# A causal convolution and a two-layer GELU block: both matmuls as pairs of 64-row tiles, the convolution moved to VectorE

## The chip, the cores and the metric

The kernel runs on one core of one Trainium2 chip. A core has a matrix engine (TensorE, "PE" in the profile, with its weight loads listed apart as "PEld"), a vector engine (VectorE, "DVE"), a scalar engine with function tables (ScalarE, "ACT"), a general engine (GpSimd, "POOL") and a queue engine that issues transfers (SyncE, "SP"). Each runs its own list of instructions in order; they meet only through semaphores. The metric is the device time of one execution in microseconds, as the median of several runs.

## The reference

Inputs, all float32: `x` of 8 x 4096 x 192, `weight` of 8 x 7, `moe_w_in` of 192 x 2048, `moe_w_out` of 2048 x 192.

```python
w = softmax(weight, axis=-1)                    # 8 heads x 7 taps
x_pad = concatenate([zeros((B, 6, D)), x], 1)   # causal: six rows of zeros in front
# channel d belongs to head d // 24
conv[b, s, d] = sum over k of w[d // 24, k] * x_pad[b, s + k, d]
h = conv.reshape(32768, 192) @ moe_w_in
g = 0.5 * h * (1 + erf(h / sqrt(2)))            # exact GELU
out = (g @ moe_w_out).astype(float32)           # 32768 x 192
```

So every token (a row of 192 channels) is mixed with the six before it in its sequence, head by head, and then goes through 192 -> 2048 -> GELU -> 192. The two matmuls hold nearly all the arithmetic.

## The kernel before, in words

The 32768 tokens go through in 64 blocks of 512 (`TB`), and a block in four tiles of 128 tokens. The order of all work is written out by hand: each engine has one list, and the blocks are software-pipelined within it.

*Load.* SP loads a block of x (384 KB) into one of three buffers `x_tok`, 128 tokens on the partitions (line 435), and stores finished output blocks (line 441). POOL casts each tile to bf16 (`x_tokb`, line 163).

*Convolution.* It is done by TensorE. At the start, VectorE builds for each of the 8 heads a banded matrix `S_ext` of 128 x 256 that holds the seven taps along its diagonals (lines 231 and 233), out of a shifted identity `bigI2` and the softmax weights. For a tile of 128 tokens `conv_st` runs, for each head, one matmul with the tile (line 363) and one with the tile before it, for the six tokens that reach back (line 373). The 24 channels of a head are the columns of the weight load, and four heads go to four column tiles of 32 (`tile_position=(0, 32 * jj)`). The result has channels on the partitions: 24 of each 32, four heads in each of two halves. ScalarE copies it as bf16 to `x2T` (line 299).

*Matmul 1.* For each 128 of the 2048 hidden units (`i` = 0..15) two matmuls add into one accumulator `hp` of 128 x 512: `winTA` with the first four heads and `winTB` with the other four (lines 395 and 402). Both use all 128 rows of the array, of which 4 x 24 = 96 hold data and the others zeros, as in `x2T`.

*GELU.* ScalarE takes a sigmoid of 1.5957... times `hp` into `tT` (line 313), and VectorE multiplies `tT` with `hp` into `gT`, bf16 (line 245): the sigmoid form that stands in for the exact GELU. There are four `hp` accumulators.

*Matmul 2.* For each tile of 128 tokens, 16 matmuls of 192 columns (line 341) add up over the 2048 hidden units; `gT` is the weight side, `woutT` streams. VectorE copies the 128 x 192 sums out (lines 258 and 272).

*Order on TensorE.* In block `bb`, behind each matmul-1 step `i` from 2 on stand four matmuls of matmul 2 of the block before; two tiles of the next block's convolution stand behind step 3, and two behind step 11. Matmul 1 waits for the multiply four steps back (`S_MULT`), the convolution for POOL's cast (`S_XCAST`) and ScalarE's copy (`S_EVAC`), matmul 2 for VectorE's copy out (`S_OCPY`).

*Start.* POOL clears six buffers, then issues the load of the tap weights (line 132) and of both weight matrices. VectorE and ScalarE compute the softmax on one partition (lines 182 to 209), TensorE spreads it over the partitions (line 326), VectorE copies that (line 219) and builds `S_ext`, and only then the first convolution and the first matmul 1 start.

Of the kernel before, what the change touches and what calls it, by code (L numbers as in the profile page):

```python
# [9 lines left out]

SIG_ALPHA = 1.5957691216057308


def bass_lightweight_conv__then__act_gelu_exact_kernel(
# [12 lines left out]
    GRP = D // H  # L27
    assert H == 8 and GRP == 24 and KS == 7
    NTOK = B * SEQ
    TB = 512  # L30
    assert NTOK % TB == 0 and SEQ % TB == 0
    NB = NTOK // TB
    NST = NTOK // 128
    STB = SEQ // 128
    NF = F // 128
    assert NF % 2 == 0
    NCH = NF
    NWDMA = 9

    NX = 3  # L40
    R = 8
    RT = 4
    HZ = 4
# [17 lines left out]

    with es:
        S_ext = sbt("S_ext", [128, H * 256], BF16)
        winTA = sbt("winTA", [128, F], BF16)
        winTB = sbt("winTB", [128, F], BF16)
        woutT = sbt("woutT", [128, NF * C], BF16)
        bigI2 = sbt("bigI2", [128, 448], BF16)
        wsb = sbt("wsb", [1, 64], F32)
        wmax = sbt("wmax", [1, 8], F32)
        wsh = sbt("wsh", [1, 64], F32)  # L70
        wex = sbt("wex", [1, 64], F32)
        wsum = sbt("wsum", [1, 8], F32)
        winv = sbt("winv", [1, 8], F32)
        wrow = sbt("wrow", [1, 64], F32)
        ones1 = sbt("ones1", [1, 128], F32)
        wbc = sbt("wbc", [128, 64], F32)
        x_tok = [sbt("x_tok%d" % i, [128, 4 * D], F32) for i in range(NX)]
        x_tokb = [sbt("x_tokb%d" % i, [128, D], BF16) for i in range(R)]
        x2T = [sbt("x2T%d" % i, [128, 2 * TB], BF16) for i in range(2)]
        tT = [sbt("tT%d" % i, [128, TB], BF16) for i in range(RT)]  # L80
        gT = [sbt("gT%d" % i, [128, NF * TB], BF16) for i in range(2)]
        o_sb = [sbt("o_sb%d" % i, [128, 4 * C], F32) for i in range(2)]
        pc = [pst("pc%d" % i, [128, 256]) for i in range(2)]
        hp = [pst("hp%d" % i, [128, TB]) for i in range(HZ)]
        obk = [pst("obk%d" % i, [128, 192]) for i in range(2)]
        S_WDMA = sem("S_WDMA")
        S_WSB = sem("S_WSB")
        S_POOLP = sem("S_POOLP")
        S_DVEP = sem("S_DVEP")
        S_ACTP = sem("S_ACTP")  # L90
        S_PEP = sem("S_PEP")
        S_XDMA = [sem("S_XDMA%d" % i) for i in range(NX)]
        S_ODMA = [sem("S_ODMA%d" % i) for i in range(2)]
        S_XCAST = sem("S_XCAST")
        S_CONV = sem("S_CONV")
        S_EVAC = sem("S_EVAC")
        S_MM1P = sem("S_MM1P")
        S_SIG = sem("S_SIG")
        S_MULT = sem("S_MULT")
        S_MM2S = sem("S_MM2S")  # L100
        S_OCPY = sem("S_OCPY")
# [3 lines left out]
        def ap(t, off, pat):  # L105
            return bass.AP(t, off, pat)

        def x_dram_ap(bb):
            return ap(xt, bb * TB * D, [[D, 128], [128 * D, 4], [1, D]])

        def out_dram_ap(bb):
            return ap(outt, bb * TB * C, [[C, 128], [128 * C, 4], [1, C]])

        def xtok_ap(slot):
            return ap(x_tok[slot], 0, [[4 * D, 128], [D, 4], [1, D]])

        def osb_ap(slot):
            return ap(o_sb[slot], 0, [[4 * C, 128], [C, 4], [1, C]])

        POOLP_MEMSETS = 6  # L120
        POOLP_TOTAL = POOLP_MEMSETS + 1

        @block.gpsimd
        def _(g):
            g.memset(winTA[:, :], 0.0).then_inc(S_POOLP)  # L125
            g.memset(winTB[:, :], 0.0).then_inc(S_POOLP)  # L126
            g.memset(bigI2[:, :], 0.0).then_inc(S_POOLP)
            g.memset(ones1[:, :], 1.0).then_inc(S_POOLP)
            g.memset(x2T[0][:, :], 0.0).then_inc(S_POOLP)
            g.memset(x2T[1][:, :], 0.0).then_inc(S_POOLP)  # L130
            g.wait_ge(S_POOLP, POOLP_MEMSETS)
            g.dma_start(
                wsb[0:1, 0 : H * KS], ap(wt, 0, [[H * KS, 1], [1, H * KS]])
            ).then_inc(S_WSB, 16)
            g.affine_select(
                out=bigI2[:, 6:134],
                in_=bigI2[:, 6:134],
                compare_op=ALU.not_equal,
                fill=1.0,
                base=0,  # L140
                pattern=[[-1, 128]],
                channel_multiplier=1,
            ).then_inc(S_POOLP)
            for j in range(4):
                g.dma_start(  # L145
                    winTA[32 * j : 32 * j + GRP, :],
                    ap(wint, GRP * j * F, [[F, GRP], [1, F]]),
                ).then_inc(S_WDMA, 16)
            for j in range(4):
                g.dma_start(  # L150
                    winTB[32 * j : 32 * j + GRP, :],
                    ap(wint, (4 * GRP + GRP * j) * F, [[F, GRP], [1, F]]),
                ).then_inc(S_WDMA, 16)
            g.dma_start(
                ap(woutT, 0, [[NF * C, 128], [C, NF], [1, C]]),
                ap(woutt, 0, [[C, 128], [128 * C, NF], [1, C]]),
            ).then_inc(S_WDMA, 16)
            for s in range(NST):
                bb, j = divmod(s, 4)
                g.wait_ge(S_XDMA[bb % NX], 16 * (bb // NX + 1))  # L160
                if s >= R:
                    g.wait_ge(S_CONV, s - R + 2)
                g.tensor_copy(  # L163
                    x_tokb[s % R][:, :], x_tok[bb % NX][:, j * D : (j + 1) * D]
                ).then_inc(S_XCAST)

        dvep = [0]

        def dve_inc(ins):
            ins.then_inc(S_DVEP)  # L170
            dvep[0] += 1
            return dvep[0]

        dve_final = []

        @block.vector
        def _(v):
            dve_inc(v.memset(pc[0][:, :], 0.0))
            dve_inc(v.memset(pc[1][:, :], 0.0))
            v.wait_ge(S_WSB, 16)  # L180
            cnt = dve_inc(
                v.tensor_reduce(  # L182
                    wmax[0:1, 0:H],
                    ap(wsb, 0, [[64, 1], [KS, H], [1, KS]]),
                    mybir.AxisListType.X,
                    ALU.max,
                )
            )
            v.wait_ge(S_DVEP, cnt)
            for h in range(H):  # L190
                cnt = dve_inc(
                    v.tensor_scalar(  # L192
                        wsh[0:1, KS * h : KS * h + KS],
                        wsb[0:1, KS * h : KS * h + KS],
                        wmax[0:1, h : h + 1],
                        None,
                        ALU.subtract,
                    )
                )
            v.wait_ge(S_ACTP, H)  # L200
            cnt = dve_inc(
                v.tensor_scalar(wsum[0:1, 0:H], wsum[0:1, 0:H], 1e-9, None, ALU.add)
            )
            v.wait_ge(S_DVEP, cnt)
            cnt = dve_inc(v.reciprocal(winv[0:1, 0:H], wsum[0:1, 0:H]))
            v.wait_ge(S_DVEP, cnt)
            for h in range(H):
                cnt = dve_inc(
                    v.tensor_scalar(  # L209
                        wrow[0:1, KS * h : KS * h + KS],  # L210
                        wex[0:1, KS * h : KS * h + KS],
                        winv[0:1, h : h + 1],
                        None,
                        ALU.mult,
                    )
                )
            assert cnt == 21
            v.wait_ge(S_PEP, 1)
            cnt = dve_inc(v.tensor_copy(wbc[:, 0 : H * KS], obk[0][:, 0 : H * KS]))
            v.wait_ge(S_DVEP, cnt)  # L220
            v.wait_ge(S_POOLP, POOLP_TOTAL)
            last = None
            for k in range(KS):
                if k > 0:
                    v.wait_ge(S_DVEP, cnt)
                for h in range(H):
                    dst = S_ext[:, 256 * h : 256 * h + 256]
                    src = bigI2[:, k : k + 256]
                    scl = wbc[:, KS * h + k : KS * h + k + 1]
                    if k == 0:  # L230
                        last = v.tensor_scalar(dst, src, scl, None, ALU.mult)  # L231
                    else:
                        last = v.scalar_tensor_tensor(  # L233
                            dst, src, scl, dst, op0=ALU.mult, op1=ALU.add
                        )
                cnt = dve_inc(last)
            dve_final.append(cnt)
            for bb in range(NB + 1):
                if bb < NB:
                    for i in range(NCH):  # L240
# [240 lines left out]
```

## Time and profile before

| | |
|---|---|
| median of 3 runs | 913.42 us (912.57 to 913.61) |
| span of the profiled execution, first to last instruction | 910.8 us; the median lies 2.6 us above it |
| TensorE matmul busy | 869.3 us (95%) |
| VectorE busy | 757.2 us (83%) |
| ScalarE busy | 645.3 us (71%) |
| GpSimd busy | 97.0 us (11%) |
| moved by DMA | 53.54 MB, 59 GB/s over the span |
| granted TensorE clock | 1.000 |

How to read it: matmuls are pipelined, so the busy time of one overlaps its neighbour's, and the distance between the starts of two tells what one costs. The chain of waits follows the work that ended last back to the start and says on which engine the time lay. A group of instructions is given as line, engine, operation, what it writes and reads, its shape and its count, then busy time and the mean of one in ns, then the idle time of the engine in front of it and what ended most of that. A timeline row is start, length, engine, line, operation, and the number of instructions merged into it. A row of the windows view has the window, its length, each engine's busy time with its instruction count, then the granted clock, the busy share of the DMA engines and GB/s.

### The profile page before, as it was taken

How to read it: one execution, taken by the hardware profiler on the slowest of the kernel's cores; microseconds unless marked ns; L12 is line 12 of the kernel's file. 1: busy time of each engine (PE TensorE's matmuls, PEld its weight loads, DVE VectorE, ACT ScalarE, POOL GpSimd, SP SyncE). 2: the span in 40 equal slices, each digit the busy share in tenths (PEclk: the TensorE clock that was granted, in tenths of full speed). 3: DMA queues.
4: the chain of work that ended last, by engine and by line, in shares of the span. 5: the costliest groups of instructions: out<-in, count | busy, mean ns of one | idle time of the engine just before them, and what ended most of it. 6: DMA issues, size and time to landing. Idle time of an engine off the chain costs nothing.

```text
span 910.8 us, 25284 instructions
## 1 busy us (share of the span) xinstructions
PE 869.3 (95%) x10178; PEld 590.0 (65%) x10178; DVE 757.2 (83%) x1358; ACT 645.3 (71%) x1298; POOL 97.0 (11%) x277
## 2 busy tenths in 40 slices
PE   0399999999999999999999999999999999999998
PEld 0156666666666666666666666666666666666666
DVE  5788888888888888888888888888888888888886
ACT  1377777777777777777777777777777777777774
POOL 6001011011101101101101101101110110110000
PEclk9999999999999999999999999999999999999999
DMA  8002212211221221221221221221122122122111
GB/s 153 4 4 69 71 47 60 71 55 53 72 63 44 71 71 36 72 70 37 71 71 39 68 71 48 60 71 54 52 71 65 42 72 70 37 71 71 36 36 54
DMA packets 70181, 53.54 MB, mean 59 GB/s; under 512 B 4336, under 2 KB 69872, under 8 KB 70064
## 3 DMA queue, kind: packets, MB, share of 16 engines
q1 hardware_dynamic: 67584, 50.34, 18.9%
q0 software_dynamic: 2480, 1.57, 1.3%
q8 instruction: 81, 1.33, 0.6%
q14 instruction: 36, 0.29, 0.1%
HBM read 28.31 MB, written 25.17 MB: 59 GB/s over the span
## 4 chain that ended last, share of the span: by engine, by line
PE 94%; DVE 4%; ACT 1%; POOL 1%; issue 0%; DMA 0%; ACTq 0%; POOLq 0%
PE obk L341 37%; PE hp L395 25%; PE hp L402 24%; PE pc L363 5%; PE pc L373 3%; DVE S_ext L233 2%; DVE gT L245 1%; ACT tT L313 0%; DVE S_ext L231 0%; ACT x2T L299 0%; POOL winTA L125 0%; DMA wsb<-in_weight_dram 0%; POOL winTB L126 0%; ACT wex L285 0%; DVE wrow L209 0%
## 5 line engine op out<-in xcount | busy, mean ns | idle before, releaser
L245 DVE TENSOR_TENSOR gT<-tT,hp 128x512 bf16<-128x512 bf16 x1024 | 684.1, 685 | 135.3 <-ACT tT L313 115.7
L313 ACT ACTIVATE tT<-hp 128x512 bf16<-128x512 f32 x1024 | 598.6, 599 | 221.2 <-PE hp L402 217.3
L341 PEld LDWEIGHTS obk<-woutT,gT 128*128 128x128 bf16 x4096 | 364.9, 98 | 209.2 <-issue 0.7
L341 PE MATMUL obk<-woutT,gT 128*128 128x192 bf16 x4096 | 482.3, 246 | 0.5 <-DVE gT L245 0.5
L395 PE MATMUL hp<-x2T,winTA 128*128 128x512 bf16 x1024 | 390.2, 381 | 1.6 <-ACT x2T L299 1.0
L402 PE MATMUL hp<-x2T,winTB 128*128 128x512 bf16 x1024 | 388.8, 380 | 0.0
L163 POOL CAST x_tokb<-x_tok 128x192 bf16<-128x192 f32 x256 | 84.9, 347 | 767.5 <-PE pc L373 478.5
L395 PEld LDWEIGHTS hp<-x2T,winTA 128*128 128x128 bf16 x1024 | 100.0, 98 | 35.2 <-DVE gT L245 3.7
L299 ACT ACTIVATE x2T<-pc 120x256 bf16<-120x256 f32 x256 | 97.5, 381 | 25.7 <-PE pc L363 25.2
L402 PEld LDWEIGHTS hp<-x2T,winTB 128*128 128x128 bf16 x1024 | 100.4, 98 | 16.0 <-issue 0.8
L363 PE MATMUL pc<-S_ext,x_tokb 128*24 128x128 bf16 x2048 | 74.0, 222 | 22.2 <-DVE S_ext L233 22.0
L258 DVE COPY o_sb<-obk 128x192 f32<-128x192 f32 x251 | 88.2, 351 | 0.0
L363 PEld LDWEIGHTS pc<-S_ext,x_tokb 128*24 128x24 bf16 x2048 | 50.8, 92 | 43.0 <-DVE S_ext L233 22.2
L373 PE MATMUL pc<-S_ext,x_tokb 128*24 128x128 bf16 x1984 | 72.3, 220 | 0.0
L373 PEld LDWEIGHTS pc<-S_ext,x_tokb 128*24 128x24 bf16 x1984 | 55.6, 93 | 0.0
L233 DVE SCALAR_TENSOR_TENSOR S_ext<-bigI,wbc,S_ext 128x256 bf16<-128x256 bf16 x48 | 19.5, 481 | 0.2
L326 PE MATMUL obk<-wrow,ones 1*128 1x56 f32 x2 | 0.7, 436 | 13.7 <-DVE wrow L209 13.7
L326 PEld LDWEIGHTS obk<-wrow,ones 1*128 1x128 f32 x2 | 0.5, 308 | 13.7 <-DVE wrow L209 13.7
L285 ACT ACTIVATE wex<-wsh 1x7 f32<-1x7 f32 x8 | 1.5, 193 | 8.1 <-DVE wsh L192 8.1
L182 DVE TENSOR_REDUCE wmax<-wsb 1x8 f32<-1x56 f32 x1 | 0.2, 199 | 7.3 <-DMA wsb<-in_weight_dram 7.3
L272 DVE COPY o_sb<-obk 128x192 f32<-128x192 f32 x5 | 1.8, 356 | 4.3 <-PE obk L341 4.3
L145 POOL DMA_DIRECT2D winTA<-in_moe_w_in_dram x4 | 2.0, 508 | 0.0
(25 smaller groups left out, 20.4 us busy)
## 6 DMA issues: line engine op xcount, KB each, us to landing
x_tok<-in_x_dram SPq DMA_DIRECT2D x64, 384.0 KB, 4.0
out_dram<-o_sb SPq DMA_DIRECT2D x64, 384.0 KB, 2.9
woutT<-in_moe_w_out_dram POOLq DMA_DIRECT2D x1, 768.0 KB, 11.6
winTA<-in_moe_w_in_dram POOLq DMA_DIRECT2D x4, 96.0 KB, 2.8
winTB<-in_moe_w_in_dram POOLq DMA_DIRECT2D x4, 96.0 KB, 4.6
wsb<-in_weight_dram POOLq DMA_DIRECT2D x1, 0.2 KB, 1.8
```

Of the source, the lines that this page charges most:

```text
L145: g.dma_start(winTA[32 * j : 32 * j + GRP, :], ap(wint, GRP * j * F, [[F, GRP], [1, F]]),).then_inc(S_WDMA, 16)
L163: g.tensor_copy(x_tokb[s % R][:, :], x_tok[bb % NX][:, j * D : (j + 1) * D]).then_inc(S_XCAST)
L233: last = v.scalar_tensor_tensor(dst, src, scl, dst, op0=ALU.mult, op1=ALU.add)
L245: v.tensor_tensor(gT[bb % 2][:, i * TB : (i + 1) * TB], tT[u % RT][:, :], hp[u % HZ][:, :], ALU.mult,).then_inc(S_MULT)
L258: v.tensor_copy(o_sb[tb % 2][:, jj * C : (jj + 1) * C], obk[s % 2][0:128, 0:C],).then_inc(S_OCPY)
L299: a.activation(out=ap(x2T[tb % 2], j * 128, [[2 * TB, 120], [TB, 2], [1, 128]]), in_=ap(pc[s % 2], 0, [[256, 120], [128, 2], [1, 128]]), f ...
L313: a.activation(out=tT[u % RT][:, :], in_=hp[u % HZ][:, :], func=AF.Sigmoid, scale=SIG_ALPHA,).then_inc(S_SIG)
L341: ins = t.matmul(obk[s % 2][0:128, 0:C], gT[bo % 2][:, i * TB + jj * 128 : i * TB + (jj + 1) * 128], woutT[:, i * C : (i + 1) * C], start= ...
L363: last = t.matmul(outp, lhs, S_ext[:, 256 * h : 256 * h + 128], start=True, stop=batch_start, tile_position=(0, 32 * jj),)
L373: last = t.matmul(outp, lhsp, S_ext[:, 256 * h + 128 : 256 * h + 256], start=False, stop=True, tile_position=(0, 32 * jj),)
L395: t.matmul(hp[z][:, 0:TB], winTA[:, 128 * i : 128 * i + 128], x2T[q][:, 0:TB], start=True, stop=False,)
L402: ins = t.matmul(hp[z][:, 0:TB], winTB[:, 128 * i : 128 * i + 128], x2T[q][:, TB : 2 * TB], start=False, stop=True,)
```

## The change

The program is rewritten around a pair of token blocks. The 32768 tokens are cut into two halves of 16384; a superblock `n` (32 of them) is 512 tokens of the first half together with the 512 at the same place in the second. The first half's channels lie on partitions 0 to 63 and the second half's on 64 to 127; the 192 channels are three slices `p` of 64.

- *Load.* SP loads x in four transfers per superblock, each to 32 partitions; per token 160 of the 192 columns are read, once from column 0 and once from column 32, so that 32 x 32 blocks stand where the transposes need them.
- *Transposes and convolution.* VectorE transposes in 32 x 32 blocks, fp32, to channels on partitions (`trans`, three instructions of 128 x 512) and then does the seven taps on 128 x 512 in fp32 (`conv`: per slice one scaling and six multiply-adds, with the tap weight as a per-partition scalar). The last tap writes bf16 `xc`. GpSimd copies the six columns that reach back (or clears them at a sequence's start). The banded matrices, the convolution's matmuls, the cast and ScalarE's copy are gone.
- *Matmul 1.* For each 128 hidden units: three slices x two halves, each a matmul of 64 rows and 512 columns at `tile_position=(0, 0)` or `(64, 0)`, into the two halves of an accumulator of 128 x 1024; two such accumulators.
- *GELU.* One table GELU of ScalarE on 128 x 1024 into `gT`; the sigmoid and VectorE's multiply are gone.
- *Matmul 2.* The 128 hidden units of a chunk are cut into rows 0 to 63 and 64 to 127, as two matmuls of 64 rows and 192 columns. Of a pair one works on one 128-token tile and one on another, in two accumulators `ob`; in a second phase (`ph`) they change places. VectorE copies two tiles out at once (`evac`).
- *Order.* On TensorE a step `i` is the six matmuls of matmul 1 and eight pairs of matmul 2 of the superblock before. On VectorE the 24 operations of the next superblock's convolution are cut into 9, 8 and 7, with an `evac` of the superblock before behind each part and one ahead of the first.
- *Start.* The tap weights are the first transfer on SP; the softmax works on 8 partitions at once; a selection matrix spreads it over the partitions through three small matmuls.

The core of the diff (declarations, the start and most removed lines are left out):

```diff
+            for n in range(NSB):
+                dst = ap(xT[n % 2], 0, [[NP * XW, 128], [XW, NP], [1, HL]])
+                if n >= 2:
+                    g.wait_ge(S_CV, NCV * (n - 1))
+                if n % SPB == 0:
+                    g.memset(dst, 0.0).then_inc(S_HALO)
+                else:
+                    g.wait_ge(S_TR, NP * n)
+                    g.tensor_copy(
+                        dst,
+                        ap(xT[(n - 1) % 2], TB, [[NP * XW, 128], [XW, NP], [1, HL]]),
+                    ).then_inc(S_HALO)
...
+            def trans(n, p):
+                if p == 0:
+                    v.wait_ge(S_XIN[n % NX], 64 * (n // NX + 1))
+                    if n >= 2:
+                        v.wait_ge(S_CV, NCV * (n - 1))
+                    if n >= 1:
+                        v.wait_ge(S_HALO, n)
+                v.transpose(
+                    ap(xT[n % 2], p * XW + HL, [[NP * XW, 128], [1, TB]]),
+                    ap(xin[n % NX], 64 * p, [[MB * XC, 128], [XC, MB], [1, 32]]),
+                ).then_inc(S_TR)
+
+            def conv(n, k, p):
+                if k == 0 and p == 0:
+                    v.wait_ge(S_TR, NP * (n + 1))
+                    v.wait_ge(S_HALO, n + 1)
+                idx = NCV * n + NP * k + p
+                if idx >= NP:
+                    v.wait_ge(S_CV, idx - NP + 1)
+                src = ap(xT[n % 2], p * XW + k, [[NP * XW, 128], [1, TB]])
+                w = wcol[:, p * KS + k : p * KS + k + 1]
+                a = acc[:, p * TB : (p + 1) * TB]
+                if k == 0:
+                    ins = v.tensor_scalar(a, src, w, None, ALU.mult)
+                else:
+                    dst = a
+                    if k == KS - 1:
+                        dst = xc[n % 2][:, p * TB : (p + 1) * TB]
+                        if n >= 2 and p == 0:
+                            v.wait_ge(S_MM1, NF * (n - 1))
+                    ins = v.scalar_tensor_tensor(
+                        dst, src, w, a, op0=ALU.mult, op1=ALU.add
                     )
...
+            for op in ops0:
+                run(0, op)
+            for n in range(NSB + 1):
+                ops = list(ops0) if n + 1 < NSB else []
+                cut = [0, 9, 17, 24, 24]
+                if n >= 2:
+                    evac(n - 2, 3)
+                for q in range(4):
+                    for op in ops[cut[q] : cut[q + 1]]:
+                        run(n + 1, op)
+                    if n >= 1 and q < 3:
+                        evac(n - 1, q)
+            evac(NSB - 1, 3)
...
                     a.activation(
-                        out=tT[u % RT][:, :],
-                        in_=hp[u % HZ][:, :],
-                        func=AF.Sigmoid,
-                        scale=SIG_ALPHA,
-                    ).then_inc(S_SIG)
+                        out=gT[n % 2][:, i * 2 * TB : (i + 1) * 2 * TB],
+                        in_=hp[u % 2][:, :],
+                        func=AF.Gelu,
+                    ).then_inc(S_GELU)
...
+            def mm1(n, i):
+                u = n * NF + i
+                if u >= 2:
+                    t.wait_ge(S_GELU, u - 1)
+                if i == 0:
+                    t.wait_ge(S_CV, NCV * (n + 1))
...
+                for p in range(NP):
+                    for hf in range(2):
+                        r = slice(64 * hf, 64 * hf + 64)
+                        ins = t.matmul(
+                            hp[u % 2][:, hf * TB : (hf + 1) * TB],
+                            win[r, p * F + 128 * i : p * F + 128 * i + 128],
+                            xc[n % 2][r, p * TB : (p + 1) * TB],
+                            start=(p == 0),
+                            stop=(p == NP - 1),
+                            tile_position=(64 * hf, 0),
                         )
...
+            def mm2_run(m, g, ph, i0, i1):
+
+
+                if g >= 2 or m >= 1:
+                    if ph == 0 and i0 == 0:
+                        t.wait_ge(S_EV, 4 * m + g - 1)
+                if ph == 1 and i0 == 0:
+                    t.wait_ge(S_PH, 4 * m + g + 1)
+                for i in range(i0, i1):
+                    for hf in range(2):
+                        sub = ph ^ hf
+                        s = 2 * g + sub
+                        r = slice(64 * hf, 64 * hf + 64)
+                        c0 = i * 2 * TB + s * 128
+                        ins = t.matmul(
+                            ob[g % 2][:, 512 * sub : 512 * sub + C],
+                            gT[m % 2][r, c0 : c0 + 128],
+                            wout[r, i * C : (i + 1) * C],
+                            start=(ph == 0 and i == 0),
+                            stop=(ph == 1 and i == NF - 1),
+                            tile_position=(64 * hf, 0),
+                        )
...
+            for n in range(NSB):
+                for i in range(NF):
+                    mm1(n, i)
+                    if n >= 1:
+                        if n == 1 and i == 0:
+                            t.wait_ge(S_WOUT, 16)
+                        if i < 2:
+                            t.wait_ge(S_GELU, NF * (n - 1) + 8 * (i + 1))
+                        g, r = divmod(i, 4)
+                        mm2_run(n - 1, g, r // 2, 8 * (r % 2), 8 * (r % 2) + 8)
...
+            def load(n):
+                if n >= NX:
+                    sp.wait_ge(S_TR, NP * (n - NX + 1))
+                for q in range(4):
+                    off = ((q // 2) * HALF + n * TB) * D + 32 * (q % 2)
+                    sp.dma_start(
+                        ap(xin[n % NX], 32 * q * MB * XC, [[MB * XC, 32], [XC, MB], [1, XC]]),
+                        ap(xt, off, [[D, 32], [32 * D, MB], [1, XC]]),
+                    ).then_inc(S_XIN[n % NX], 16)
```

517 lines of the change are left out of this document (162 added, 355 removed).

## The prediction

> **What bounds the kernel now.** I read the page's busy shares and chain first, then the costliest groups.
>
> ```profile
> span 910.8 us, 25284 instructions
> PE 869.3 (95%) x10178; PEld 590.0 (65%) x10178; DVE 757.2 (83%) x1358; ACT 645.3 (71%) x1298; POOL 97.0 (11%) x277
> ...
> PE 94%; DVE 4%; ACT 1%; POOL 1%; issue 0%; DMA 0%; ACTq 0%; POOLq 0%
> ...
> L245 DVE TENSOR_TENSOR gT<-tT,hp 128x512 bf16<-128x512 bf16 x1024 | 684.1, 685 | 135.3 <-ACT tT L313 115.7
> L313 ACT ACTIVATE tT<-hp 128x512 bf16<-128x512 f32 x1024 | 598.6, 599 | 221.2 <-PE hp L402 217.3
> L341 PEld LDWEIGHTS obk<-woutT,gT 128*128 128x128 bf16 x4096 | 364.9, 98 | 209.2 <-issue 0.7
> ```
>
> TensorE sets the end: 94% of the chain is PE, and the idle gaps of DVE and ACT end on each other or on PE. A matmul's busy time overlaps its neighbour's, so I price matmuls by the distance between starts, from the timeline:
>
> ```profile
> 402.35 0.38 PE L395 MATMUL hp<-x2T,winTA 128*128 128x512 bf16 x1
> 402.56 0.38 PE L402 MATMUL hp<-x2T,winTB 128*128 128x512 bf16 x1
> 402.78 0.38 PE L395 MATMUL hp<-x2T,winTA 128*128 128x512 bf16 x1
> ...
> 404.40 0.49 PE L341 MATMUL obk<-woutT,gT 128*128 128x192 bf16 x4
> ...
> 404.94 0.24 PE L363 MATMUL pc<-S_ext,x_tokb 128*24 128x128 bf16 x4
> 405.00 0.24 PE L373 MATMUL pc<-S_ext,x_tokb 128*24 128x128 bf16 x4
> 405.06 0.24 PE L363 MATMUL pc<-S_ext,x_tokb 128*24 128x128 bf16 x4
> ...
> 405.40 0.39 PE L395 MATMUL hp<-x2T,winTA 128*128 128x512 bf16 x1
> ...
> 901.90 5.24 PEld L341 LDWEIGHTS obk<-woutT,gT 128*128 128x128 bf16 x64 [0.71 <-issue]
> ```
>
> A 512-column matmul takes 0.215 us (402.35 to 402.78, two of them). A 192-column one takes (5.24 - 0.098) / 63 = 0.0816 us, its 98 ns weight load hidden under the stream ahead. The convolution costs, per pair of 128-token tiles, 405.40 - 404.40 - 4 x 0.0816 = 0.67 us. Per 512 tokens: 32 x 0.215 + 64 x 0.0816 + 2 x 0.67 = 6.88 + 5.22 + 1.34 = 13.44 us. As a check, the windows view of line 402 alone:
>
> ```profile
> 100.00:800.00 700.00, 313.92 (x829) 81.08 (x828) 1.00 0.21 60
> ```
>
> 829 / 16 = 51.8 blocks in 700 us, 13.51 us each: the sum is 0.5% short, and I carry that.
>
> **PE after the change.** A superblock is 2 x 512 tokens. Matmul 1 is now 16 x 3 x 2 matmuls of 512 columns with 64 rows, matmul 2 is 256 of 192 columns. What they cost depends on whether the two row tiles of a pair stream together. If so, a pair costs one matmul: 48 x 0.215 + 128 x 0.0816 = 10.32 + 10.44 = 20.77 us, with the 0.5% 20.87. This replaces 2 x 13.51 = 27.0: the gain is 2.7 us from the convolution leaving PE and 3.4 us from matmul 1, which loses its zero rows (three passes over 64 + 64 full rows for two over 128 rows with 96 filled, on twice the tokens: 48 streams for 64). Matmul 2 gains nothing. If not, a pair costs two matmuls, 41.7 us. No row tile stands in this trace; column tiles do. In the lines at 404.94 to 405.06, four 128-column matmuls on four 32-column tiles start every 0.058 us, and one of 128 columns would need 0.0816 x 128/192 = 0.054. So four tiles stream in the time of one, with eight instructions issued in 58 ns, where matmul 2 needs four in 82. I take full overlap, and keep two matmuls as the other end.
>
> The weight loads double per streamed column: two per 0.0816 us. Two rows bound them:
>
> ```profile
> L363 PEld LDWEIGHTS pc<-S_ext,x_tokb 128*24 128x24 bf16 x2048 | 50.8, 92 | 43.0 <-DVE S_ext L233 22.2
> ```
>
> A load of 24 columns lasts 92 ns and one of 128 columns 98, so nearly all of it is latency. If two loads cannot overlap at all, a pair of matmul 2 is at most 2 x 0.0816 = 0.163 us (one load per 0.0816 is shown). I take 0.0816.
>
> [...]
>
> **ACT.** The multiply and the sigmoid become one GELU of 1024 columns. Slope from two rows, here and above:
>
> ```profile
> L299 ACT ACTIVATE x2T<-pc 120x256 bf16<-120x256 f32 x256 | 97.5, 381 | 25.7 <-PE pc L363 25.2
> ```
>
> (599 - 381) / 256 = 0.852 ns an element, so 599 + 512 x 0.852 = 1035 ns, 16.6 us a superblock (proportional at most, 1198: 19.2). Both lie below 20.87. Matmul 1 waits for the GELU two steps back: a step of PE is 1.30 us, so that GELU has 0.65 x 3 = 1.95 us after its matmul, and needs some 0.2 + 1.04. Cover 0.7 us a step. The new wait between the two halves of a group of matmul 2 has a step of matmul 1 in front of it, 0.65 us against a drain of some 0.2; everything on PE stands behind it, but it has been served by then. In the first superblock there is no matmul 2, and ACT sets the pace.
>
> **DVE** loses the 685 ns multiply and gains transposes, taps and wider evictions.
>
> ```profile
> 14.69 1.92 DVE L231 TENSOR_SCALAR S_ext<-bigI,wbc 128x256 bf16<-128x256 bf16 x8
> ...
> L258 DVE COPY o_sb<-obk 128x192 f32<-128x192 f32 x251 | 88.2, 351 | 0.0
> L233 DVE SCALAR_TENSOR_TENSOR S_ext<-bigI,wbc,S_ext 128x256 bf16<-128x256 bf16 x48 | 19.5, 481 | 0.2
> ...
> 19.93 3.27 DVE S_ext L233 x8
> ```
>
> A tap of 256 elements is 3.27 / 8 = 0.409 us. From COPY (192: 351 ns) to TENSOR_TENSOR (512: 685 ns) an element costs 1.04 ns, so a tap of 512 is 0.409 + 0.267 = 0.676; bounds 0.676 and twice the lone duration, 0.962. The scaling first tap: twice 0.24, 0.48 (0.24 to 0.68). The fp32 transpose has no row; nearest is COPY, one tensor in and one out: 0.351 + 320 x 0.00104 = 0.684 (0.5 to 0.96). Eviction of 2 x 192: 0.55. Per superblock 3 x 0.684 + 3 x 0.48 + 18 x 0.676 = 15.7 for the convolution, plus 4 x 0.55: 17.9 us, under 20.87. A wait for a tap three ops back is served while two ops are queued, so free. The four evictions wait for matmul 2 in the middle of the taps. The last one, queued ahead of the next superblock's transposes, comes when PE ends a superblock. So the next convolution starts there and is due one superblock later: 0.55 + 15.7 + two evictions 1.1 = 17.35, cover 3.5 us, gone if a tap takes 0.87. Eviction 1, which frees the accumulator for group 3 at 12 steps = 15.6 us, is done at about 13.1.
>
> **SP, POOL and the queues.** POOL's cast goes; POOL copies six columns per superblock, and the transposes that wait for the copy (and all taps behind them) come a superblock later. x now goes in four DMAs of 328 KB per superblock, 42 MB for 25, because 160 of 192 columns are read twice.
>
> ```profile
> 4.00:6.00 2.00, 0.00 (x0) 0.00 (x0) 0.00 (x0) 0.00 (x0) 2.00 (x5) 1.00 0.99 302
> 10.00:12.00 2.00, 0.00 (x0) 0.00 (x0) 0.27 (x3) 1.63 (x16) 2.00 (x5) 1.00 0.79 113
> ...
> x_tok<-in_x_dram SPq DMA_DIRECT2D x64, 384.0 KB, 4.0
> ```
>
> 1.31 MB is 4.3 us at 302 GB/s, and 13.7 at 384 KB per 4.0 us: below a superblock. On SP a load stands behind a store that waits for eviction 1, and is still issued over one superblock ahead. Nothing charged.
>
> **Start and end.**
>
> ```profile
> 6.91 0.63 POOL L132 DMA_DIRECT2D wsb<-in_weight_dram  x1 [0.30 <-POOL x2T L130]
> 8.72 0.20 DVE L182 TENSOR_REDUCE wmax<-wsb 1x8 f32<-1x56 f32 x1 [7.30 <-DMA wsb<-in_weight_dram]
> 14.44 0.22 DVE L219 COPY wbc<-obk 128x56 f32<-128x56 f32 x1 [0.76 <-PE obk L326]
> ...
> 39.11 0.58 PE L395 MATMUL hp<-x2T,winTA 128*128 128x512 bf16 x1 [0.58 <-ACT x2T L299]
> ...
> 907.40 0.36 DVE L272 COPY o_sb<-obk 128x192 f32<-128x192 f32 x1 [0.96 <-PE obk L341]
> ```
>
> Today matmul 1 starts at 39.1, behind six memsets, the weights (14.7) and 1.92 + 6 x 3.27 = 21.5 us of building the Toeplitz matrices. After: the weights' DMA is the first on SP and lands near 2.6 (1.8 us, 6.91 to 8.72); the softmax takes at most 14.66 - 8.72 = 5.9, so ready by 8.5. The first 1.31 MB of x, sharing the engines with w_in (half of 302 GB/s), lands near 10.5 (6 to 14). Convolution 15.7: matmul 1 at 26.2 us. First superblock, ACT-paced: 0.65 + 0.2 + 15 x 1.035, to 42.5; the second convolution (26.2 + 15.7) is ready at 41.9. Then 31 x 20.87 = 647.0, to 689.5. Tail: the last GELU 0.6 (1.04 + 0.2, less the half step of matmul 2 that covers it), matmul 2 128 x 0.0816 = 10.45, drain and eviction 0.9, store 3.1 (907.76 to 910.8): 704.5. The median 913.4 lies 2.6 above the span of 910.8, so 707. For another superblock time P: 49.7 + 31.5 P.
>
> **Rivals.**
>
> Slower: the row tiles of a pair run one after the other, so the change halves the work per stream and doubles the streams. P = 41.7, the first superblock 4 us longer: 1368 us. For it: no row tile in the trace; against it: the four column tiles above. It decides from P = 27.4 (913.4), a pair costing 1.31 matmuls. Beside it, the slower form with loads: each tile's weights go in only after its stream: 48 x (0.215 + 0.098) + 128 x (0.0816 + 0.098) = 38.0, 1247 us. [...]
>
> Part overlap: a pair costs 1.03 to 1.31 matmuls, or the loads of matmul 2 go one after the other (0.122, midway: P = 26.0, 869). 730 to 913. For it: two loads per 82 ns are shown nowhere except with 24 columns. [...]
>
> DVE becomes the bound: with taps at 0.82 (twice 0.409), transposes at 0.96 and first taps at 0.68 it needs 21.9 a superblock, and each of the two opening convolutions grows 4 us: 50.5 + 679 + 15 + 2.6 = 747; with 0.962 for taps and for all six other ops 859. For it: no fp32 tap and no transpose in the trace. Against: no DVE row is slower than 1.04 ns an element beyond its fixed part.
>
> **Chances.** Full overlap as summed 0.72 (own range 695 to 730: start 6 to 14, steps up to 2% longer); DVE-bound 0.09; part overlap 0.08; no overlap 0.07; load after stream 0.02; the rest 0.02. A change under 0.2% is about what a measurement here cannot tell. Faster 0.89, same 0.01, slower 0.10. Range 690 to 830: it holds the first case, most of the DVE case and half of part overlap.
>
> **What would show it.** Right: the two matmuls of a pair start within a few ns, pairs every 0.215 and 0.082 us, the chain all PE, mean tap near 0.7 us, GELU near 1.04 us, matmul 1 from about 26 us. Wrong: pairs 0.43 and 0.163 apart (no overlap); weight loads that end matmul 2's waits; PE idle at the first matmul of a superblock on a tap of line `conv` (DVE); PE waiting for GELU inside a superblock (ACT).

## The result

| | median | lowest to highest | runs |
|---|---|---|---|
| before | 913.0 us | 912.37 to 913.61 | 4 |
| changed | 712.68 us | 712.42 to 715.25 | 4 |

The ratio is 0.7812, 95% interval 0.7799 to 0.7825: 200 us less. The forecast was 707 us, own range 695 to 730. The page of the changed kernel (span and busy time, chain, costliest groups):

```profile
span 710.9 us, 24500 instructions
PE 676.3 (95%) x11270; PEld 487.9 (69%) x11270; DVE 544.5 (77%) x901; ACT 526.2 (74%) x516; POOL 18.2 (3%) x44
...
PE 94%; DVE 2%; DMA 2%; ACT 2%; issue 0%; SPq 0%; DVEq 0%
PE ob L311 47%; PE hp L287 46%; DMA xin<-in_x_dram 2%; ACT gT L256 2%; DVE acc L202 1%; DVE xT L179 0%; SPq L348 0%; DVE acc L195 0%; DVE xc L202 0%; DVE osb L211 0%; SPq L341 0%; DVEq L174 0%
...
L256 ACT ACTIVATE gT<-hp 128x1024 bf16<-128x1024 f32 x512 | 523.2, 1023 | 169.1 <-PE hp L287 169.1
L202 DVE SCALAR_TENSOR_TENSOR acc<-xT,wcol,acc 128x512 f32<-128x512 f32 x480 | 325.6, 747 | 0.0
L211 DVE COPY osb<-ob 128x384 f32<-128x384 f32 x128 | 71.0, 555 | 148.2 <-PE ob L311 148.2
L179 DVE STREAM_TRANSPOSE xT<-xin 128x512 f32<-128x512 f32 x96 | 60.4, 681 | 9.7 <-DMA xin<-in_x_dram 9.7
```

TensorE is still 94% of the chain. It has only less to stream: 676 us busy for 869. VectorE's idle time in front of its evictions (148 us) ends on TensorE, so VectorE waits for PE and not the other way round; TensorE waits for a tap only once, at its first matmul 1 (25.1 us, shown below). The timeline of one superblock, first TensorE and then VectorE (start, length, engine, line, operation, count):

```profile
402.26 0.82 PE L311 MATMUL ob<-wout,gT 64*128 64x192 bf16 x16
402.93 0.81 PE L287 MATMUL hp<-xc,win 64*128 64x512 bf16 x6
403.57 0.66 PE L311 MATMUL ob<-wout,gT 64*128 64x192 bf16 x12
...
423.85 0.81 PE L287 MATMUL hp<-xc,win 64*128 64x512 bf16 x6
```

```profile
403.13 0.56 DVE L211 COPY osb<-ob 128x384 f32<-128x384 f32 x1 [3.92 <-PE ob L311]
403.61 1.89 DVE L179 STREAM_TRANSPOSE xT<-xin 128x512 f32<-128x512 f32 x3
405.53 1.28 DVE L195 TENSOR_SCALAR acc<-xT,wcol 128x512 f32<-128x512 f32 x3
406.72 2.07 DVE L202 SCALAR_TENSOR_TENSOR acc<-xT,wcol,acc 128x512 f32<-128x512 f32 x3
...
409.18 5.38 DVE L202 SCALAR_TENSOR_TENSOR acc<-xT,wcol,acc 128x512 f32<-128x512 f32 x8
...
417.59 2.08 DVE L202 SCALAR_TENSOR_TENSOR xc<-xT,wcol,acc 128x512 bf16<-128x512 f32 x3
419.57 0.55 DVE L211 COPY osb<-ob 128x384 f32<-128x384 f32 x1
424.05 0.56 DVE L211 COPY osb<-ob 128x384 f32<-128x384 f32 x1 [3.92 <-PE ob L311]
```

Superblocks start on TensorE at 402.93 and 423.85: 20.92 us each. Six matmuls of matmul 1 take 403.57 - 402.93 = 0.64 us, three streams of 512 columns, not six; sixteen of matmul 2 take 402.93 - 402.26 = 0.67, eight streams of 192. The convolution begins when TensorE ends a superblock (the eviction at 403.13) and its last tap ends at 419.67, 4.2 us ahead of its use at 423.85.

The opening, from the timeline and the chain of the changed kernel:

```profile
14.84 1.90 DVE L179 STREAM_TRANSPOSE xT<-xin 128x512 f32<-128x512 f32 x3 [9.67 <-DMA xin<-in_x_dram]
...
30.06 7.26 PE L287 MATMUL hp<-xc,win 64*128 64x512 bf16 x36 [25.10 <-DVE xc L202]
30.46 0.15 PEld L287 LDWEIGHTS hp<-xc,win 64*128 64x128 bf16 x2 [0.27 <-issue]
30.89 0.15 PEld L287 LDWEIGHTS hp<-xc,win 64*128 64x128 bf16 x2 [0.28 <-issue]
...
47.27 0.82 PE L287 MATMUL hp<-xc,win 64*128 64x512 bf16 x6 [0.20 <-ACT gT L256]
...
696.42 10.51 PEld L311 LDWEIGHTS ob<-wout,gT 64*128 64x128 bf16 x256 [0.69 <-ACT gT L256]
```

Matmul 1 starts at 30.06 us instead of 39.11, later than forecast, because the first x lands at 14.7 us. The first superblock's matmul 1 then takes until 47.27.

### The profile page after: what moved, and what is told of

Same layout as the page of the kernel before. It is cut to its first block, busy times and chain, and to the rows that moved or that the text cites. A ratio compares the mean times of both kernels' runs of the same rounds, so it can differ in the third digit from the quotient of the medians.

```text
span 710.9 us, 24500 instructions
## 1 busy us (share of the span) xinstructions
PE 676.3 (95%) x11270; PEld 487.9 (69%) x11270; DVE 544.5 (77%) x901; ACT 526.2 (74%) x516; POOL 18.2 (3%) x44
## 4 chain that ended last, share of the span: by engine, by line
PE 94%; DVE 2%; DMA 2%; ACT 2%; issue 0%; SPq 0%; DVEq 0%
PE ob L311 47%; PE hp L287 46%; DMA xin<-in_x_dram 2%; ACT gT L256 2%; DVE acc L202 1%; DVE xT L179 0%; SPq L348 0%; DVE acc L195 0%; DVE xc L202 0%; DVE osb L211 0%; SPq L341 0%; DVEq L174 0%
## 5 line engine op out<-in xcount | busy, mean ns | idle before, releaser
L256 ACT ACTIVATE gT<-hp 128x1024 bf16<-128x1024 f32 x512 | 523.2, 1023 | 169.1 <-PE hp L287 169.1
L287 PE MATMUL hp<-xc,win 64*128 64x512 bf16 x3072 | 417.7, 378 | 26.9 <-DVE xc L202 25.1
L311 PEld LDWEIGHTS ob<-wout,gT 64*128 64x128 bf16 x8192 | 352.6, 94 | 118.2 <-ACT gT L256 0.7
L311 PE MATMUL ob<-wout,gT 64*128 64x192 bf16 x8192 | 419.2, 243 | 0.5 <-ACT gT L256 0.5
L202 DVE SCALAR_TENSOR_TENSOR acc<-xT,wcol,acc 128x512 f32<-128x512 f32 x480 | 325.6, 747 | 0.0
L287 PEld LDWEIGHTS hp<-xc,win 64*128 64x128 bf16 x3072 | 141.3, 94 | 97.3 <-DVE xc L202 25.2
L211 DVE COPY osb<-ob 128x384 f32<-128x384 f32 x128 | 71.0, 555 | 148.2 <-PE ob L311 148.2
L179 DVE STREAM_TRANSPOSE xT<-xin 128x512 f32<-128x512 f32 x96 | 60.4, 681 | 9.7 <-DMA xin<-in_x_dram 9.7
L202 DVE SCALAR_TENSOR_TENSOR xc<-xT,wcol,acc 128x512 bf16<-128x512 f32 x96 | 66.4, 749 | 0.0
L195 DVE TENSOR_SCALAR acc<-xT,wcol 128x512 f32<-128x512 f32 x96 | 40.9, 483 | 1.1
```

What stands on the lines that cost most here:

```text
L179: v.transpose(ap(xT[n % 2], p * XW + HL, [[NP * XW, 128], [1, TB]]), ap(xin[n % NX], 64 * p, [[MB * XC, 128], [XC, MB], [1, 32]]),).then_i ...
L195: ins = v.tensor_scalar(a, src, w, None, ALU.mult)
L202: ins = v.scalar_tensor_tensor(dst, src, w, a, op0=ALU.mult, op1=ALU.add)
L211: v.tensor_copy(ap(osb[m % 2], 2 * g * C, [[8 * C, 128], [C, 2], [1, C]]), ap(ob[g % 2], 0, [[1024, 128], [512, 2], [1, C]]),).then_inc(S_EV)
L256: a.activation(out=gT[n % 2][:, i * 2 * TB : (i + 1) * 2 * TB], in_=hp[u % 2][:, :], func=AF.Gelu,).then_inc(S_GELU)
L287: ins = t.matmul(hp[u % 2][:, hf * TB : (hf + 1) * TB], win[r, p * F + 128 * i : p * F + 128 * i + 128], xc[n % 2][r, p * TB : (p + 1) * T ...
```

## Do the two row tiles stream side by side?

The theory: a pair of 64-row matmuls costs one stream, and the gain rests on it. The rivals: the gain comes from elsewhere, or each tile's weights cannot be loaded while it streams.

```diff
                         s = 2 * g + sub
-                        r = slice(64 * hf, 64 * hf + 64)
+                        r = slice(0, 64)
 ...
-                            tile_position=(64 * hf, 0),
+                            tile_position=(0, 0),
```

> The changed kernel with both matmuls of each pair of matmul 2 on rows 0 to 63 (the lower hidden units of each chunk are summed twice, the upper ones left out); same instructions, loads, columns and waits. If the gain rests on the two row tiles streaming side by side, a pair of matmul 2 now costs two streams: 32 x 10.45 us more, 713 + 334 = about 1047 us, and the tail of 256 matmuls takes 20.9 us instead of 10.5. If the tiles did not run side by side, nothing changes: 713. If a tile's weights go in only after its own stream (98 ns each), a matmul costs 0.18 us: the tail takes 46 us and the whole about 1850.

Measured 1050.8 us, 338 more for 334 expected. The timeline at the end, where the tail follows the last step:

```profile
1022.48 22.59 PEld L311 LDWEIGHTS ob<-wout,gT 64*128 64x128 bf16 x272
```

272 loads in 22.59 us are 0.083 us each, the price of one stream of 192 columns per matmul instead of half of one (256 in 10.51 before). Two things follow. On one tile the matmuls run one after the other, so side by side they do save a whole stream (for matmul 1, which this run leaves alone, the 0.64 us for six matmuls show the same). And in this run a tile's loads, 94 ns each, stay hidden under its own stream; loaded behind it, they would make a matmul cost 0.0816 + 0.094 = 0.18.

How cheap are the loads? The next edit shortens the streams and leaves the loads:

```diff
+                        nc2 = C if i == 0 else 64
                         ins = t.matmul(
-                            ob[g % 2][:, 512 * sub : 512 * sub + C],
+                            ob[g % 2][:, 512 * sub : 512 * sub + nc2],
                             gT[m % 2][r, c0 : c0 + 128],
-                            wout[r, i * C : (i + 1) * C],
+                            wout[r, i * C : i * C + nc2],
```

> Matmul 2 streams only 64 of the 192 columns, but for the first chunk of each group (the other output columns are left out); the weight loads stay as they are, two per pair. It prices the loads, which the prediction bounded between nothing and one per stream. If the loads are free, a pair costs 0.027 us, PE needs 14 us a superblock, and VectorE becomes the bound with some 17.2: about 30 + 16.5 + 31 x 17.2 + 9 + 2 = 590 us, and the tail's 256 matmuls take about 3.8 us. If two loads of a pair go one after the other and each takes 27 ns or more, the tail takes 7 us or more; at 82 ns each it stays at 21. In any case below 713 unless the loads were the bound already.

Measured 580.65 us. The chain and the start of the tail:

```profile
DVE 78%; issue 10%; ACT 5%; PE 4%; DMA 2%; SPq 0%; DVEq 0%
...
569.36 2.14 PEld L312 LDWEIGHTS ob<-wout,gT 64*128 64x128 bf16 x128 [1.01 <-ACT gT L256]
```

The 128 loads belong to 64 pairs, four of them with 192 columns. (2.14 - 0.09 - 4 x 0.082) / 60 = 0.029 us a pair: two loads of 128 columns fit into 29 ns, near the 27 of the stream alone. The loads were nowhere near the bound. The chain has moved to VectorE (78%), the next limit: in this run's timeline two superblocks start on TensorE at 282.45 and 299.35, 16.90 us apart, each after a wait for the last tap.

## In which order may the tiles' matmuls stand?

```diff
-                for p in range(NP):
-                    for hf in range(2):
+                for hf in range(2):
+                    for p in range(NP):
```

> Matmul 1 with its six matmuls ordered by half: three on rows 0 to 63, then three on rows 64 to 127, instead of alternating; the same work. If matmuls start in the order of the program, the second tile starts only when the third matmul of the first one starts, 0.43 us late, and a step of 1.30 us grows by 0.215 to 0.43: 110 to 220 us more, 823 to 933. If TensorE may take the other tile's matmul out of order, nothing changes: 713.

Measured 714.66 us: no change to speak of, so the second theory. The timeline, and the windows view of line 287 alone (window, length, PE and PEld busy, granted clock, DMA share, GB/s):

```profile
402.21 0.82 PE L287 MATMUL hp<-xc,win 64*128 64x512 bf16 x6
402.86 0.57 PE L311 MATMUL ob<-wout,gT 64*128 64x192 bf16 x9
```

```profile
402.10:402.30 0.20, 0.09 (x2) 0.17 (x4) 1.00 1.27 243
```

The six take 402.86 - 402.21 = 0.65 us as before, and two of them run in the first 0.09 us, where a stream lasts 0.215: the other tile's first matmul, fourth in the program, does not wait for the two in front of it. How far that reaches:

```diff
-                for i in range(i0, i1):
-                    for hf in range(2):
+                for hf in range(2):
+                    for i in range(i0, i1):
```

> The changed kernel with each run of 16 matmuls of matmul 2 ordered by half: eight on rows 0 to 63, then eight on rows 64 to 127 (in the tail 16 and 16); the same work. Ordering the six of matmul 1 so changed nothing, so a tile's matmuls can start ahead of the other tile's earlier ones in the program. If each tile takes its own matmuls from a deep queue, nothing changes again: 713 to 715. If TensorE looks only about three matmuls ahead, the second tile starts some five matmuls late: 0.3 to 0.4 us a step lost at one or both changes of tile, 500 steps: 150 to 250 us more, 860 to 960.

Measured 737.95 us, 25 more, which neither expectation had. The timeline of a few steps, and of the tail:

```profile
400.88 0.33 PE L311 MATMUL ob<-wout,gT 64*128 64x192 bf16 x2
400.97 0.38 PE L287 MATMUL hp<-xc,win 64*128 64x512 bf16 x1
401.04 0.76 PE L311 MATMUL ob<-wout,gT 64*128 64x192 bf16 x11
401.57 0.39 PE L287 MATMUL hp<-xc,win 64*128 64x512 bf16 x1
401.64 0.33 PE L311 MATMUL ob<-wout,gT 64*128 64x192 bf16 x2
...
715.85 16.40 PEld L311 LDWEIGHTS ob<-wout,gT 64*128 64x128 bf16 x256 [0.65 <-ACT gT L256]
```

The tail, with 16 matmuls on one tile and then 16 on the other, takes 16.4 us: side by side 10.5, one after the other 20.9. Each of the 16 runs then takes 16.4 / 16 = 1.025 us where alone it would take 16 x 0.0816 = 1.306; the next run starts 0.28 us before, which is 3.4 matmuls. The single records of the trace show it directly: at the first change of tile a matmul starts out of the row at 716.86 us, and three of the first tile start after it (716.93, 717.02 and 717.10). So in this run the other tile's matmul starts about three matmuls ahead of its place (the second theory), but my price for it, 150 to 250 us, was six to ten times too high: in a step the other matmul's work fills the hole. While one tile ends its eight of matmul 2, the other is already in the next matmul 1 (the matmul 1 at 401.57 between those of matmul 2), and a step takes 1.34 us instead of 1.31. 31 x 16 x 0.037 + 5.9 in the tail = 24. With row tiles, then, TensorE did not start its matmuls strictly in the order of the program in these two runs (two at once in the first 0.09 us; 3.4 matmuls early), and it is not quite true that every engine runs its list in order.

## What each part of the change is worth

The convolution on TensorE, in the kernel before (the stages of later blocks taken out; POOL's cast is kept on its own semaphore):

```diff
-                    if bb + 1 < NB and i in (4, 5, 12, 13):
-                        act_evac({4: 0, 5: 1, 12: 2, 13: 3}[i], bb + 1)
...
-                    q = bb % 2
+                    q = 0
...
-                    if bb + 1 < NB and i == 3:
-                        conv_st(4 * (bb + 1) + 0)
-                        conv_st(4 * (bb + 1) + 1)
-                    if bb + 1 < NB and i == 11:
-                        conv_st(4 * (bb + 1) + 2)
-                        conv_st(4 * (bb + 1) + 3)
```

> The kernel before with the convolution of the first block alone: all later blocks multiply with that block's result, so 63 of 64 convolutions on TensorE and their copies on ScalarE are left out; loads and casts stay. It prices what moving the convolution off TensorE is worth. By the prediction's 0.67 us per pair of tiles: 63 x 1.34 = 84 us less, 913 - 84 = 829. If the convolution's column tiles hid in gaps that PE has anyway, less than 30 us go; if switching between tile shapes costs more than the gaps show, more than 100.

Measured 829.4 us, 84 less than 913.4: the price of 0.67 us per pair of tiles holds. The table GELU alone, in the kernel before:

```diff
-                        func=AF.Sigmoid,
-                        scale=SIG_ALPHA,
-                    ).then_inc(S_SIG)
+                        func=AF.Gelu,
+                    ).then_inc(S_MULT)
```

(writing to `gT`, with VectorE's multiply taken out)

> The kernel before with one part of the change alone: ScalarE's table GELU on each 128x512 accumulator straight into gT; the sigmoid and VectorE's multiply are gone, all else stays. TensorE was busy without a gap in the steady blocks, so taking 684 us off VectorE gives nothing there; only the few waits on the multiply at start and end go: 905 to 913. If the multiply was co-critical (VectorE busy 83%), some 30 us or more go: below 885.

Measured 911.43 us, ratio 0.9983 (0.9973 to 0.9992). The page and the waits:

```profile
PE 868.0 (96%) x10178; PEld 590.4 (65%) x10178; DVE 117.0 (13%) x334; ACT 644.8 (71%) x1298; POOL 97.5 (11%) x277
...
DVE o_sb L249 <- PE obk L331: 771.9, 251, 17.7
```

VectorE falls from 757 to 117 us busy and the time hardly moves. The GELU's part in the change is to clear VectorE for the convolution. No run shows this by itself, but the sum is plain: a superblock would need 32 multiplies, which in the kernel before start no less than some 0.6 us apart (405.08 and 405.67 us), so about 19 us, beside some 15 us of transposes and taps, and only 20.9 are there.

The rest of the steady gain is matmul 1. A superblock costs 20.92 us for 2 x 13.51 = 27.02: 6.1 less, of which 84 / 31.5 = 2.67 is the convolution and 3.4 is left, as 16 fewer streams of 0.215 us make it. This last part is a difference, not a run of its own.

## How much room VectorE has

```diff
+            def extra(n):
+                for e in range(NX_TAPS):
+                    c = NX_TAPS * (n - 2) + e
+                    if c >= 3:
+                        v.wait_ge(S_DMY, c - 2)
+                    src = ap(xT[n % 2], (e % NP) * XW, [[NP * XW, 128], [1, TB]])
+                    v.scalar_tensor_tensor(
+                        dmy[c % 3][:, :], src, wcol[:, 0:1], src,
+                        op0=ALU.mult, op1=ALU.add,
+                    ).then_inc(S_DMY)
```

called ahead of the last taps, with `NX_TAPS` 6 and 12.

> The changed kernel with six more multiply-adds of 128x512 in fp32 per superblock on VectorE, ahead of the last taps, from the third superblock on; their result is thrown away. In the trace the last tap ends about 4.2 us before the next superblock starts, and a tap takes 0.66 us: six take 4.0 us, so the time stays within 3 us of 713 (up to 716). If VectorE were as critical as TensorE, 30 x 4.0 = 119 us more: 832.

Six: 715.54 us, ratio 0.7834 (0.7821 to 0.7847), 2.9 us more. 119 us more of VectorE work are hidden. Its timeline:

```profile
399.80 4.06 DVE L193 SCALAR_TENSOR_TENSOR dmy<-xT,wcol 128x512 f32<-128x512 f32 x6
...
420.80 4.06 DVE L193 SCALAR_TENSOR_TENSOR dmy<-xT,wcol 128x512 f32<-128x512 f32 x6
```

VectorE now works without a pause from one superblock to the next, 21.00 us each, against TensorE's 20.92: it has no room left.

> As with six more taps, but twelve, 7.9 us per superblock. Past a cover of 4.2 us the rest shows: 30 x 3.7 = 111 us more, about 824. If VectorE were co-critical, 30 x 7.9 = 237 more, 950; if it still hides, 713.

Twelve: 892.65 us, 180 more, where the cover alone predicts 111. The windows view of this run around one start of a superblock (window, length, busy time of PE, PEld, DVE, ACT, POOL, granted clock, DMA share, GB/s), and its timeline:

```profile
400.00:411.70 11.70, 11.70 (x198) 8.72 (x194) 11.70 (x19) 9.15 (x10) 0.00 (x0) 1.00 0.78 146
411.70:415.30 3.60, 0.07 (x4) 0.05 (x4) 3.56 (x6) 0.45 (x1) 0.00 (x0) 0.82 0.01 4
415.30:420.30 5.00, 5.00 (x44) 3.50 (x46) 4.96 (x10) 1.98 (x2) 0.45 (x1) 0.50 0.25 82
```

```profile
415.28 1.47 PE L304 MATMUL hp<-xc,win 64*128 64x512 bf16 x6 [3.53 <-DVE xc L219]
416.51 1.51 PE L328 MATMUL ob<-wout,gT 64*128 64x192 bf16 x16
...
421.24 0.84 PE L328 MATMUL ob<-wout,gT 64*128 64x192 bf16 x16
...
423.42 0.56 DVE L228 COPY osb<-ob 128x384 f32<-128x384 f32 x1 [2.25 <-PE ob L328]
```

TensorE stalls 3.53 us for the convolution, and comes back at a granted clock of 0.50 for about 5 us: the first five half-steps (six matmuls of matmul 1 or sixteen of matmul 2 each) take 421.24 - 415.28 = 5.96 us instead of 5 x 0.654 = 3.27. These 2.7 us do not stay on TensorE. VectorE's first eviction waits for step 3 of matmul 2 (2.25 us idle at 423.42), in front of the rest of the taps, so the late start also delays the next convolution. A full such superblock takes 27.32 us (415.28 to the next start at 442.60). VectorE is idle in it for these 2.25 us only, so its own work is 25.07 us, 4.15 more than the 20.92; that and the idle time make the 6.4 us. Over the 30 it came to 6.0.

The same run has four superblocks that start behind a stall as long, but at the full clock, and they set the two parts apart:

```profile
74.45 0.82 PE L304 MATMUL hp<-xc,win 64*128 64x512 bf16 x6 [3.53 <-DVE xc L219]
...
99.44 0.99 PE L304 MATMUL hp<-xc,win 64*128 64x512 bf16 x6 [3.89 <-DVE xc L219]
```

```profile
74.40:79.40 5.00, 4.95 (x82) 3.76 (x84) 4.96 (x10) 3.24 (x4) 0.45 (x1) 1.00 0.25 82
```

Behind the stall at 74.45 the clock is 1.00, and that superblock takes 99.44 - 74.45 = 24.99 us, 4.07 above 20.92. So VectorE's work beyond its room costs 4.1 us a superblock, where 3.7 were expected: the idle time that the twelve taps (8.04 us) could fill is the 3.92 us in front of the eviction, not 4.2. The clock of 0.50 adds 27.32 - 24.99 = 2.3 us. 30 x 4.1 = 123 of the 180 us are VectorE's work, and most of the other 57 are the clock. TensorE is busy 746.4 us here for 676.3, and the 70 us more are 26 times the 2.7: all but those four of the 30. The gap of 3.53 us at 415.28 has a clock of 0.50 behind it, the equal gap at 74.45 one of 1.00, so a gap of this length alone does not decide it. What does, no run here shows.

## The opening

```diff
+            g.wait_ge(S_XIN[0], 64)
             for c0, c1, s in ((0, FC, S_WIN[0]), (FC, F, S_WIN[1])):
...
             load(0)
+            sp.wait_ge(S_XIN[0], 64)
             load(1)
```

> The changed kernel with the first superblock's x alone on the DMA engines: the loads of the second and third and of both weight matrices wait until it has landed. In the trace it lands at 14.7 us, 12 us after it begins, while weights and later blocks move beside it. If that sharing is what made it late, it lands near 8 us (1.31 MB at 216 GB/s is 6.1 us), everything after it moves up by 6 to 7 us: 706 to 707. If 32-partition transfers of 640-byte rows are slow by themselves, it lands no earlier than 12: 710 to 713. If the weights, now later, become the wait, TensorE stalls in the first superblock and the time does not fall.

Measured 709.69 us, ratio 0.7772 (0.7761 to 0.7784): 3.0 us less, half of what was expected. The timeline:

```profile
10.35 1.90 DVE L180 STREAM_TRANSPOSE xT<-xin 128x512 f32<-128x512 f32 x3 [5.23 <-DMA xin<-in_x_dram]
...
14.58 1.28 DVE L196 TENSOR_SCALAR acc<-xT,wcol 128x512 f32<-128x512 f32 x3 [2.33 <-POOL xT L147]
```

and the windows view of the same run, while that load is alone on the DMA engines:

```profile
6.00:8.00 2.00, 0.00 (x0) 0.00 (x0) 0.00 (x0) 0.00 (x0) 0.00 (x0) 1.00 1.21 199
```

The transposes start at 10.35 instead of 14.84, 4.5 us earlier. Alone, the load moves 199 GB/s, not the 302 of the kernel before with 128 partitions and 768-byte rows. So sharing made up 4.5 us of the delay; the lower rate is another 2.3 (1.31 MB at 199 instead of 302 GB/s). Then 2.33 us are lost again to a new wait: GpSimd clears the leading columns of the first superblock behind the transfers that it now issues late. So matmul 1 starts 2.2 us earlier (27.84); the other 0.8 us lies in the first superblock, which takes 16.43 us here and 17.2 before. In the next run that clearing goes ahead:

```diff
+            g.memset(
+                ap(xT[0], 0, [[NP * XW, 128], [XW, NP], [1, HL]]), 0.0
+            ).then_inc(S_HALO)
+            g.wait_ge(S_XIN[0], 64)
...
-            for n in range(NSB):
+            for n in range(1, NSB):
```

> As with the first superblock alone on the DMA engines, and GpSimd clears the six leading columns of the first superblock before it issues the weights' transfers instead of behind them. In the run without that the first taps waited 2.33 us for that clearing. If it was only the order in GpSimd's queue, these come off: 709.7 - 2.3 = 707.4 (706.8 to 708). If the first matmul then waits for w_in, which is issued at the same time as before, the gain is smaller.

Measured 708.11 us, ratio 0.7752 (0.7742 to 0.7763), the fastest that does all the work, but 0.7 us above the 707.4 and just outside the range given. The timeline:

```profile
12.31 1.28 DVE L199 TENSOR_SCALAR acc<-xT,wcol 128x512 f32<-128x512 f32 x3
...
25.57 4.90 PE L291 MATMUL hp<-xc,win 64*128 64x512 bf16 x22 [20.66 <-DVE xc L206]
...
26.38 1.90 DVE L183 STREAM_TRANSPOSE xT<-xin 128x512 f32<-128x512 f32 x3 [0.87 <-DMA xin<-in_x_dram]
```

The wait is gone and matmul 1 starts at 25.6 us; the second convolution now waits 0.87 us for its x, which is loaded later. The 0.7 us lie in the first superblock, which takes 17.07 us for 16.43 in the run before; why it varies so, no run shows.

## Why the prediction was right, point by point

*Full overlap of the pairs.* Right, and the step on which it hung. Forecast 20.87 us a superblock, measured 20.92. It was read from the column tiles of the kernel before, four matmuls in 58 ns. That was a conclusion from one kind of tile to another, which the trace could not test; the run on one tile does. The two parts of the gain on TensorE, 2.7 and 3.4 us, came out at 2.67 and 3.4.

*Weight loads.* Taken as free; the run with 64 columns shows 29 ns for two at most, the upper bound of 0.163 us a pair was far off. That a load of 24 columns and one of 128 last 92 and 98 ns, which the prediction read as latency, pointed this way.

*ACT.* GELU 1035 ns forecast, 1023 measured; it does not hold TensorE up in the steady part (from 100 to 300 us TensorE is busy for 200.00 of the 200).

*DVE.* From start to start, a tap was put at 0.676 us and takes (5.38 - 0.747) / 7 = 0.66; a transpose at 0.684 and takes (405.53 - 403.61) / 3 = 0.64; a first tap at 0.48 and takes (406.72 - 405.53) / 3 = 0.40. An eviction was put at 0.55 and lasts 0.555. The cover came out at 4.2 us for the 3.5 forecast, and the runs with more taps bracket it: six taps (4.0 us) hide, twelve do not. The prediction had the cover end where a tap takes 0.87 us. It did not have what lies beyond: a stall of 3.53 us with a granted clock of 0.50 behind it.

*Start.* Here a term was mis-sized. The first x was to land at 10.5 us (6 to 14) from 302 GB/s halved; it landed at 14.7, outside the bounds, and matmul 1 started at 30.06 instead of 26.2. The rate came from a load of the kernel before with another shape; the new one moves some 200 GB/s alone. The later runs show 4.5 us of sharing in it.

*End.* From the last GELU's wait to the end of the span 710.9 - 696.4 = 14.5 us, forecast 10.45 + 0.9 + 3.1.

*The sum.* The start gives +3.9 us, 31 superblocks 31 x 0.05 = +1.6, and the first superblock +0.9 (47.27 - 30.06 = 17.2 us where the sum has 42.5 - 26.2 = 16.3): 704.5 becomes 710.9, the span. In that first superblock the pairs of matmul 1 start 0.43 us apart at first (the loads at 30.46 and 30.89), twice the 0.215 of the sum. This is about the pace that the run with twelve more taps shows at a granted clock of 0.50 (three pairs in 416.51 - 415.28 = 1.23 us), but the windows view gives 1.00 for 28 to 32 us, so the cause stays open. The 2.6 us around the span, a median less the span of one run, was 1.7 in the profiled run (712.64).

*The rivals.* No overlap and load after stream fall with the run on one tile (0.083 us a matmul on one tile, half of that on two). Part overlap falls with 20.92. DVE-bound is not the case, but it was the next one in line: with matmul 2 cut down, DVE takes 78% of the chain.

## What to carry to other kernels

Count TensorE's streams, not its multiplications: a contraction of 192 costs two streams of 128 rows, or three streams of 64 + 64 rows for twice the tokens, and the second is a quarter cheaper (48 streams of 0.215 us here for 64). Work that leaves the critical engine is worth its streams there only if the engine that takes it has room, and that room must be made first; the table GELU alone gave 0.2%, and by the sum above it made the room for a 9% step. Keep a margin in front of the critical engine: going over by 4.1 us a superblock cost 6.0 here, because behind most of the stalls the granted clock was low as well (0.50 for about 5 us at 415.28).

## What the runs showed of the hardware that was not expected

- The matmuls of the two row tiles did not have to alternate in the program: three of one tile ahead of the other's cost nothing to speak of (714.66 us for 712.68), eight ahead cost 25 us (737.95), and with 16 in a row the next tile started 0.28 us, some 3.4 matmuls, early.
- Two weight loads of 64 rows and 128 columns, one on each row tile, fitted into 29 ns beside streams of 64 columns (128 loads in 2.14 us).
- Behind a gap of 3.53 us on TensorE the granted clock was 0.50 for about 5 us (at 415.28 us); behind an equally long one in the same run it was 1.00 (at 74.45).
- Loads of 640-byte rows to 32 partitions each moved 199 GB/s with nothing beside them, against 302 GB/s for 768-byte rows to 128 partitions. Which of the two differences makes it was not tried.
